# A gated-attention and MLP kernel on one core: the second half of its hand-written instruction order arranged anew, with some steps on other engines and in other buffers

## The chip, the cores and the metric

The kernel runs on one core of one Trainium2 chip. A core has a matrix engine (PE, which loads weights and multiplies), a vector engine (DVE), a scalar engine (ACT), a general engine (POOL) and a queue engine (SP) that here only issues transfers; ACT issues a few as well. Each engine works through its own instructions strictly in order and waits for the others by semaphores. The metric is the device time of one execution in microseconds, taken as the median of the runs. Lower is better.

## The reference

Four batches, eight heads, 768 time steps, head size 48. A gated linear attention comes first, and its output, with the heads laid side by side to 384 columns, goes through a low-rank mixing along time and then a two-layer MLP with a residual:

```python
for t in range(S):
    state = alpha[:, :, t, :, None] * state + np.einsum('bhd,bhe->bhde', k[:, :, t], v[:, :, t])
    y[:, :, t] = np.einsum('bhd,bhde->bhe', q[:, :, t], state)
...
xt = x.transpose(0, 2, 1)
h = xt @ U @ V
u = x + h.transpose(0, 2, 1)
ch = np.maximum(u @ w_ch1, 0.0) @ w_ch2
return (u + ch).astype(np.float32)
```

## The kernel before

Each batch is cut into six chunks of 128 time steps. Work is named by a step's short name and "batch.chunk". One chunk of attention goes like this, for the batches 2 and 3 that the prediction speaks of; the line numbers are those of the profile:

- `load` (L350, and L343 for alpha) brings alpha, k, q and v of a chunk into one of 40 `io` buffers, all issued by SP in this part of the program.
- `ln` (ACT, L549) takes the logarithm of alpha, `cum` (PE, L561 and L570) sums it along time, two chunks at once in batch 3 and in `cum1`/`cum2` steps, and `exp` and `tot` (ACT, L601, L602, L604) make the factors `ai`, `aa` and `tot` of it.
- `rv` (a plain cast of v: L265 on ACT, L269 on POOL), `rk` and `rq` (L612 on DVE or POOL) scale k and q. They write one of four `rkq` buffers.
- `tkq` (L637) transposes both by a transfer that SP issues, into one of four `kqt` buffers. This is done for all chunks of batch 2 and for 3.0 to 3.2; the other chunks of batch 3 go through PE (`tr`, L625) and copies (`kqev`, L265 or L267).
- `sc` (PE, L653, eight matmuls) makes the scores, `mask` (DVE, L663, two of them) cuts them to the causal part, `d` (PE, L676), `add` (DVE, L703) and `st` (L687, DVE or POOL) carry the state on, `y` (PE, L715 and L720) makes the output and `yev` (L265 or L267) copies it out of PSUM.

When all six chunks of a batch are done, `xu` (PE, L735), `utx` and `xs` (L750) make the low-rank product, `hb3` (PE, L760, three chunks side by side; `hb`, L771, for one) spreads it over time, `u` (DVE, L772) adds the residual for one chunk, and `tu` (L777, issued by SP) transposes the `u` of two chunks by a transfer. Then the MLP: `mlp1 b.tt.j` (PE, L820, three matmuls; tt is the half of the time steps, j one of twelve column blocks), `relu` (L830 on ACT, L832 on DVE), `mlp2 b.c.g` (PE, L846, four matmuls), `out` (DVE, L852) and `store` (L855, L857, issued by SP).

Nothing in the program is scheduled by a compiler. The functions that describe the stages only add steps to a list of 1036 with their dependences. The string `TABLE` then gives the order: each entry of three characters is the number of a step (two characters, base 64) and the engine on which it is to run (P, A, D, G for POOL, S for SP). The string `SLOTS` gives, in the order in which buffers are first used, which of a pool's slots each one takes. A step waits for what it reads, and for the last users of the slot that it writes.

```python
op = self.ops[CODE.index(table[n]) * len(CODE) + CODE.index(table[n + 1])]
for b in op.bufs:
    if b.slot is None:
        b.slot = b.pool.slots[CODE.index(next(nxt))]
op.fn({"P": "PE", "A": "ACT", "D": "DVE", "G": "POOL", "S": "SP"}[table[n + 2]])
```

Around entry 560 the program is in the MLP of batch 1, which is the filler for PE there, while the attention of batch 2 runs through its small steps; behind it the MLP of batch 2 is laid between the attention steps of batch 3, and at the end the MLP of batch 3 stands alone.

Of the kernel before, what the change touches and what calls it, by code (L numbers as in the profile page):

```python
# [34 lines left out]
LrDLqDLsSLiPJhPLoDLmDLpSJlPNDGJiDLkDLjDJmPM+GJZPJnPNJPN3PLlSN5AJaPOFPNSGNTGCRSNjANYPJbPJoDNEGNKDMPPMJPJcDNZDNUSNFSOIAMQD
NiAMRPMbPCVSCUSOHACMSNkANhAOaAMKALxPMSALyAMcDLvPN2DL-PMADLwAOKAMDPMEDOMGN4PN6DMLPMHPMIDObAOJAMMALzPN7PN8DN9DL0ANGPNVPNWD
NHDNlGLtPNIDLuDL9PNXDL1PL+AL2AOLGCOSL7PL5PMTPMUDL8DL6ANgACNSMXPMFPMNPMODCZSCYSF+SL3PNmGMGDCSSL4AONPNrPMdPNLPNbPMBPMePCWS
MYDMZPNaGNnSNMANsDOcDOdGNtDOePOOPMaDOPANwAN+PN-DOQDOfPMCAOgAMfPCaSFzSMiPNcAOhAOGGMgDOAGOUPOZGORPGKSJpSGESF-SJwSOiPNoPOVD
OSDMjPOBPOCAMnPMoPFySNqDNpDMpPNuPNvAOjDOTDOXPOYAOkDOWGOlPMkPOmAOnPMVPMsPOoAOuPMWDJdSOvDOwPO1POxDO2DGFSOySMtPOzPO0DMuPM2P
# [7 lines left out]
DCHCEABAQCSDFBTDRDGHCVCAUEADBCAWCCBAABHEDEXYGCZFABCHaEGDFbBBADBCBBHFEDBCAGEcBFCAAHAEGAFBBBBEBdGFCDBAHABeEBfghjHBEilmkCAn
BBDAFGACADBCBAFABGCBDACCDCFBGCBBDCABBBFBGDABEGHCHAEFDBCCAHAIGDAECBFDBACAHGECAACAECJBKCGDDFAAHAEMDACBDABLDFGBEPHDCNAACBCB
BCABGBBFEOCBQSTDHARGVBACAEDADHBGFACBUAWCAaZBACEDHYDCCBCFHBeEDEFCACDbABjCHFcADAAABEDfkAgCBGBHCFAEDGCBCHCAFEDBADGBCXHEBBhA
CFAnGEEDBHFGICBBABBDADAAHAEDDGCFACEAHFDEBBACABBCECCFHDBBAECAFHBEJCFKCBBAEDHFAMBGCDEFGAEBDHEGBCAHDBCANOSGUWVE  # L50
"""


# [863 lines left out]
```

## Time and profile before

| what | us |
|---|---|
| median of 3 runs | 160.28 |
| the runs | 158.03, 161.46, 160.28 |
| the profiled execution, its own time | 157.4 |
| its span, first to last instruction | 155.6 |
| PE busy in it | 145.7 |
| DVE, ACT, POOL busy in it | 107.2, 88.3, 62.2 |

The profiled execution is faster than each of the three runs, so a sum made on its rows is about an execution that waited less than the usual one. The span and the execution's own time differ by 1.8 us that lie around the program. Times "at" a point are microseconds from the span's start.

### The profile page before, as it was taken

What the parts mean: (1) busy time and instruction counts of PE and PEld (TensorE: products, weight loads), DVE (VectorE), ACT (ScalarE), POOL (GpSimd) and SP (SyncE); (2) the same over time, 40 slices, a digit from 0 to 9 for tenths busy, and PEclk for the clock granted to TensorE, in tenths of its full rate; (3) what the DMA queues carried; (4) which work ended last, traced back from release to release, by engine and by line L of the source; (5) the groups of instructions that cost most, each with busy time, mean ns of one, the idle gap of its engine ahead of it and who ended that gap; (6) DMA issues with size and microseconds to landing.
All of it is one profiled execution on the core that took longest, in us unless ns stands there. A gap on an engine that the chain in (4) does not pass through costs nothing.

```text
span 155.6 us, 4554 instructions
## 1 busy us (share of the span) xinstructions
PE 145.7 (94%) x1773; PEld 96.4 (62%) x1773; DVE 107.2 (69%) x239; ACT 88.3 (57%) x228; POOL 62.2 (40%) x100
## 2 busy tenths in 40 slices
PE   0889999999999999999996999999999999999992
PEld 0567777766676665766674656665777566666661
DVE  6169989978975568787885879479978473313251
ACT  3858878999946673776658463864442202462000
POOL 8079787448947722292253227006641000000000
PEclk9999999999999999999999999999999999999999
DMA  4999999999999999999699997899984055872142
GB/s 119 323 328 327 293 244 361 320 261 247 283 335 289 188 239 207 236 221 201 136 193 150 237 235 142 170 187 190 215 198 115 0 101 117 256 257 83 51 156 101
DMA packets 94453, 32.35 MB, mean 208 GB/s; under 512 B 88128, under 2 KB 94400, under 8 KB 94432
## 3 DMA queue, kind: packets, MB, share of 16 engines
q1 hardware_dynamic: 89152, 30.09, 81.5%
q10 hardware_dynamic: 5280, 1.97, 4.8%
q8 instruction: 14, 0.23, 0.7%
q14 instruction: 7, 0.06, 0.1%
HBM read 23.79 MB, written 4.72 MB: 183 GB/s over the span
## 4 chain that ended last, share of the span: by engine, by line
PE 66%; DMA 16%; SPq 4%; ACT 3%; DVE 3%; POOL 3%; issue 1%; POOLq 0%
PE ps L846 27%; PE ps L820 18%; DMA h1t<-in_moe_w_ch_dram 4%; DMA io<-in_alpha_dram 4%; DMA kqt<-rkq 3%; SPq L350 3%; DMA io<-in_k_dram 2%; POOL rkq L612 2%; DMA io<-in_q_dram 2%; PE ps L421 2%; PE ps L653 2%; DVE ub L772 2%; PE ps L445 2%; PE ps L720 1%; PE ps L771 1%
## 5 line engine op out<-in xcount | busy, mean ns | idle before, releaser
L846 PE MATMUL ps<-w_sb,h1t 128*128 128x384 bf16 (+2 forms) x300 | 52.1, 320 | 0.1
L820 PE MATMUL ps<-uT,w_sb 128*128 128x384 bf16 x288 | 50.6, 326 | 0.0
L846 PEld LDWEIGHTS <-h1t 128*128 128x128 bf16 x300 | 27.6, 98 | 17.0 <-issue 1.2
L820 PEld LDWEIGHTS <-w_sb 128*128 128x128 bf16 x288 | 27.0, 98 | 16.8 <-issue 0.3
L830 ACT ACTIVATE h1t<-ps 128x384 bf16<-128x384 f32 x53 | 24.4, 497 | 21.2 <-PE ps L820 20.9
L832 DVE TENSOR_SCALAR h1t<-ps 128x384 bf16<-128x384 f32 x43 | 22.9, 554 | 17.8 <-PE ps L820 16.2
L663 DVE TENSOR_TENSOR pm<-ps,maskc 128x512 bf16<-128x512 f32 x28 | 17.6, 684 | 4.8 <-PE ps L653 4.0
L852 DVE TENSOR_TENSOR io<-ub,ps 128x384 f32<-128x384 bf16 (+2 forms) x25 | 12.8, 533 | 9.0 <-PE ps L846 8.9
L612 POOL TENSOR_TENSOR rkq<-io,aa 128x384 bf16<-128x384 f32 x12 | 11.0, 915 | 15.7 <-DMA io<-in_q_dram 15.7
L612 POOL TENSOR_TENSOR rkq<-io,ai 128x384 bf16<-128x384 f32 x10 | 9.1, 914 | 13.0 <-DMA io<-in_k_dram 5.4
L265 ACT CAST xb<-ps 128x192 bf16<-128x192 f32 (+1 forms) x23 | 8.4, 404 | 9.5 <-PE ps L720 5.9
L456 DVE TENSOR_TENSOR pm<-ps,maskp 128x512 bf16<-128x512 f32 x20 | 13.2, 683 | 0.6 <-PE ps L445 0.4
L772 DVE TENSOR_TENSOR ub<-xb,ps 128x384 bf16<-128x384 bf16 x24 | 11.8, 548 | 1.9 <-PE ps L760 1.0
L404 POOL TENSOR_TENSOR rkq<-io,aa 128x384 bf16<-128x384 f32 x9 | 8.3, 922 | 6.0 <-ACT aa L397 4.0
L687 POOL TENSOR_TENSOR st<-sm,tot 128x384 bf16<-128x384 f32 x7 | 5.8, 830 | 9.6 <-DVE sm L703 9.6
L404 POOL TENSOR_TENSOR rkq<-io,ai 128x384 bf16<-128x384 f32 x9 | 8.2, 913 | 3.0 <-ACT ai L396 2.5
L265 ACT COPY kqt<-ps 128x512 bf16<-128x512 bf16 x14 | 8.3, 592 | 1.9 <-PE ps L625 1.0
L549 ACT ACTIVATE lt<-io 128x384 bf16<-128x384 f32 x14 | 7.2, 524 | 3.1 <-DMA io<-in_alpha_dram 3.1
L267 DVE COPY kqt<-ps 128x512 bf16<-128x512 bf16 x16 | 6.6, 419 | 3.0 <-ACT lt L549 1.9
L421 PE MATMUL ps<-ident,rkq 128*128 128x128 bf16 x80 | 7.7, 229 | 0.7 <-DVE pm L456 0.4
L382 PE MATMUL ps<-lt,upto 128*128 128x384 bf16 x10 | 3.8, 382 | 4.5 <-ACT lt L373 4.5
L601 ACT ACTIVATE ai<-ps 128x384 bf16<-128x384 f32 x14 | 6.7, 508 | 1.5 <-POOL st L687 1.4
(122 smaller groups left out, 213.0 us busy)
## 6 DMA issues: line engine op xcount, KB each, us to landing
io<-in_q_dram SPq DMA_DIRECT2D x24, 192.0 KB, 4.3
io<-in_k_dram SPq DMA_DIRECT2D x22, 192.0 KB, 3.9
io<-in_alpha_dram SPq DMA_DIRECT2D x20, 192.0 KB, 4.3
io<-in_v_dram SPq DMA_DIRECT2D x20, 192.0 KB, 4.1
out_dram<-io SPq DMA_DIRECT2D x13, 192.0 KB, 2.0
io<-in_moe_w_ch_dram SPq DMA_DIRECT2D x12, 192.0 KB, 4.9
h1t<-in_moe_w_ch_dram SPq DMA_DIRECT2D x4, 576.0 KB, 7.1
out_dram<-io SPq DMA_DIRECT2D x20, 96.0 KB, 2.2
```

What stands on the lines that cost most here:

```text
L265: nc.scalar.copy(dst, src)
L404: eng.tensor_tensor(jh(dst()[:, :, 0:D]), raw(a), jh(x()), op=ALU.mult)
L421: nc.tensor.matmul(dst, lhsT=ring()[:, HP * j + 2 * a : HP * j + 2 * a + 2, :].rearrange("t h w -> t (h w)"), rhs=ident, start=True, stop= ...
L456: nc.vector.tensor_tensor(dst, s2, maskp.to_broadcast([C, 2, 2, C]), op=ALU.mult)
L612: eng.tensor_tensor(dst()[:, :, 0:D], a(), x(), op=ALU.mult)
L663: nc.vector.tensor_tensor(pm()[:, :, par, :], s2, maskc.to_broadcast([C, HP, C]), op=ALU.mult)
L772: P.add(f"u {b}.{c}", lambda e, c=c, hb=hb: nc.vector.tensor_tensor(ub()[:, c, :], xb()[:, c, :], hb()[:, 0:DM], op=ALU.add), r=[hb] + xk( ...
L820: nc.tensor.matmul(hb()[:, 0:TW], lhsT=w1_sb[:, ct, jt * 128 : (jt + 1) * 128], rhs=u_half(uT, ct, tt, b in QUEUE_U), start=(ct == 0), sto ...
L830: nc.scalar.activation(dst, hb()[:, 0:TW], AF.Relu)
L832: nc.vector.tensor_scalar_max(dst, hb()[:, 0:TW], 0.0)
L846: nc.tensor.matmul(hb()[:, 0 : hi - lo], lhsT=h1()[:, jt, c * C : (c + 1) * C], rhs=w2_sb[:, jt, lo:hi], start=(jt == 0), stop=(jt == NJ - 1),
L852: P.add(f"out_{hi - lo} {b}.{c}", lambda e, hb=hb, lo=lo, hi=hi: nc.vector.tensor_tensor(flat(ou)[:, lo:hi], ub()[:, c, lo:hi], hb()[:, 0 ...
```

## The change

Only the two strings are edited. The set of steps is the same 1036 (with the same four warm-up matmuls), and the first 560 entries are untouched; in the profiled execution entry 560 is issued at 70.2 us. Behind it the order of the steps on PE, ACT, DVE and POOL is new in three stretches: up to the `xu` step of batch 2; from there to the first `mlp1` step of batch 2; and from there, through the attention of batch 3, to the fourth `mlp1` step of batch 3. At each of these three points the same steps stand ahead on PE as before, and behind the last one PE's order is the old one. On SP the order of the transfers is the same as before throughout.

38 steps change their engine. Of those between the entry and the `xu` of batch 2: `rq 2.3`, `rk 2.4` and `st 2.2` go from DVE to POOL, `rv 2.2` and `rv 2.5` from ACT to POOL, `rv 2.3` from POOL to ACT, `st 2.1` from POOL to DVE; `yev` and `relu` steps are exchanged between ACT and DVE. Later `rk 3.3`, `st 3.2` and `rv 3.2` go to POOL, `rv 3.0` to ACT, `st 3.3` to DVE, and some twenty `relu`, `kqev` and `yev` steps change between ACT and DVE. Many buffers take other slots.

Two of the lines of the diff, one of the order and one of the slots:

```diff
-B2SGDDFxDJWDJPPJTPJFPJGAKYPJJPJUDI5PJRPJSAJKALAACDSK2DKKDI9PI+AJDPCASIxPB9SIyAKZDI1PI2AJQDKGPI6DJEDLCPKIDLGALHALVAKoPKHD
+GDDFxDJPPJQDKKDI-PI9PJTPJUDJDPJEDLAAJAAJWDKGPJJPI+AI5PKYPJKDI6AJRPIrPKHDKZDKIDJSAIsAIpPIqAJFPJGALCPLUALVALGAK2GKaDKVPKoP
...
-AcADBGCBCAAEHDdBGBCeBDFBfAHEgCChGDBiHBjBFAAEkBCDCABGBAlHmFACDEnACADACBGFBBECCDFEAGADGHIBJKMLCBOPABAFCDNAABHAAFBDCDEAFBGA
+AcADBGCBCAAEHDdBCBFeBGDBfAHCgCChEGBiHBjBDAACkBFGCABEBAlHmDACDCnAFAGACBEDBBCCFDFEAEAGGHIBJKMLCBOPABADFGNAABHAADBGFDCADBEA
```

Three places are shown in the order of the instructions, before and then after. A name with a number is a buffer; equal instructions that follow each other are one row.

The first is PE just ahead of `sc 2.5`, the scores of the last chunk of batch 2. Before, its weights and columns come from `kqt_188`, and `mlp2` matmuls (L846) stand ahead of it:

```order
L846 LDWEIGHTS h1t_73
L846 MATMUL ps<-w_sb,h1t_73 128x384
L846 LDWEIGHTS h1t_73
L846 MATMUL ps<-w_sb,h1t_73 128x384
L653 LDWEIGHTS kqt_188
L653 MATMUL ps<-kqt_188 128x128
```

After, `sc 2.5` reads `kqt_190`, and the rows ahead of it are those of `sc 2.4`, which reads `kqt_189`:

```order
L653 LDWEIGHTS kqt_189
L653 MATMUL ps<-kqt_189 128x128
L653 LDWEIGHTS kqt_189
L653 MATMUL ps<-kqt_189 128x128
L653 LDWEIGHTS kqt_190
L653 MATMUL ps<-kqt_190 128x128
```

The four `mlp2`, four `d` and four more `mlp2` matmuls that stood between the two chunks' scores are now elsewhere.

The second is POOL in the same part of the program. Before, behind `rk 2.3` (first row): `st 2.1`, `rk 2.5`, `rq 2.4`, `rv 2.3`, `rq 2.5`, `st 2.3`.

```order
L612 TENSOR_TENSOR rkq_79<-io_165,ai_181 128x8x48
L687 TENSOR_TENSOR st_198<-sm_194,tot_185 128x384
L612 TENSOR_TENSOR rkq_81<-io_140,ai_182 128x8x48
L612 TENSOR_TENSOR rkq_78<-io_135,aa_177 128x8x48
L269 CAST rv_172<-io_141 128x384
L612 TENSOR_TENSOR rkq_81<-io_142,aa_179 128x8x48
L687 TENSOR_TENSOR st_197<-sm_194,tot_184 128x384
```

After, behind the same `rk 2.3`: `rq 2.3`, `rv 2.2`, `rk 2.4`, `rk 2.5`, `rq 2.4`, `st 2.2`, `rq 2.5`, `rv 2.4`.

```order
L612 TENSOR_TENSOR rkq_79<-io_167,ai_181 128x8x48
L612 TENSOR_TENSOR rkq_79<-io_132,aa_178 128x8x48
L269 CAST rv_176<-io_134 128x384
L612 TENSOR_TENSOR rkq_81<-io_137,ai_182 128x8x48
L612 TENSOR_TENSOR rkq_78<-io_140,ai_180 128x8x48
L612 TENSOR_TENSOR rkq_81<-io_135,aa_177 128x8x48
L687 TENSOR_TENSOR st_199<-sm_195,tot_186 128x384
L612 TENSOR_TENSOR rkq_78<-io_142,aa_179 128x8x48
L269 CAST rv_173<-io_143 128x384
```

`rq 2.3`, `rv 2.2`, `rk 2.4` and `st 2.2` have come to POOL, and `rv 2.3` and `st 2.1` have left it.

The third is DVE at the end of batch 2's attention, from the copy `utx 2` on. Before, `rk 3.3` stands behind it, and the `u` steps (L772) run over the chunks 5, 4, 3, 2, 1, 0, with an `out` step of batch 1 (L852) ahead of the last two:

```order
L267 CAST utx_206<-ps 96x384
L612 TENSOR_TENSOR rkq_80<-io_150,ai_180 128x8x48
L772 TENSOR_TENSOR ub_205<-xb_202,ps 128x384 x4
L852 TENSOR_TENSOR io_162<-ub_204,ps 128x384
L772 TENSOR_TENSOR ub_205<-xb_202,ps 128x384 x2
```

After, the six `u` steps follow each other and run over the chunks 1, 2, 3, 4, 5, 0:

```order
L267 CAST utx_206<-ps 96x384
L772 TENSOR_TENSOR ub_205<-xb_202,ps 128x384 x6
L852 TENSOR_TENSOR io_162<-ub_204,ps 128x384
L687 TENSOR_TENSOR st_196<-ps,tot_185 128x384
L703 TENSOR_TENSOR sm_194<-ps,st_196 128x384
```

On PE `hb3 2.0`, which makes the sums for the chunks 0 to 2, now stands ahead of `hb3 2.3` for the chunks 3 to 5, where before it stood behind it. The order of the three transposes on SP is still `tu 2.5` (chunks 4 and 5), `tu 2.3`, `tu 2.1`.

More of the change, by code (lines that the diff above doesn't have):

```diff
@@ L30 @@
 KiAIoAK0AKEGKkAKhAKjAIjPFwPJ+AIcDIdDIePKlGKmGIkDB8SJLPJBPJHPJCAKxAJMDKFSKnSKSGKTGK1GM8AIfDKyAJNPJIDJXPKJPJVPLBAJOAJYAKUS
-B2SGDDFxDJWDJPPJTPJFPJGAKYPJJPJUDI5PJRPJSAJKALAACDSK2DKKDI9PI+AJDPCASIxPB9SIyAKZDI1PI2AJQDKGPI6DJEDLCPKIDLGALHALVAKoPKHD
-KVPKWDKqDKpDLEALUALFAKgAKaGB6SJxPJyPCBSJzPJ2PKrPI3PLWGIrPKXDK3SLJGKLPKbPJ3PIsDLIDKuPB+SLKSI4AKwGLXGKvALYSI-PJAAM7AKsDJ0D
-KMDKtDJ4PKcAI7PK7PIpPIqAI8AIzPI0AJ5DK4PNeACCSK8DM9PNAANBANOAK6DK5DM-ANPAK9GNCALLPLDGJrPLOPCLSLMDLNDLPDCJSCQSCKSJsPLZPLaD
-LbDJtPJuDLRPCGSIvPK+PLTAK-DLQGLcPItPIuDIwDLSANdANRANQALdALePLfANfPNxALgPN0ANzACESLhDCXSNyAJfPCISCTSOEAODAJgPN1DLnPCFSNNA
@@ L35 @@
[L35 to L39, printed above, removed]
@@ L40 @@
-OpPOqDOrPMqDO3SM3PM4PMxPMyPOsDMzPPkPMvDM5DPlDOtSJjSPcPPYPPZAPiPPaPPbAPjAPCPPAPPBAPQPMlDM0DPKPO8PPLDO+PO6PPGPO7APdAPRDPUP
+GDDFxDJPPJQDKKDI-PI9PJTPJUDJDPJEDLAAJAAJWDKGPJJPI+AI5PKYPJKDI6AJRPIrPKHDKZDKIDJSAIsAIpPIqAJFPJGALCPLUALVALGAK2GKaDKVPKoP
+KpDB2SCDSKgGCASLEAKXDKqDM7AJ2PJ3PI7PI8DI1PB9SLIGI2DLWGKrPLFALJGIxPKuPB6SCBSKsDKWDKvAKwALHAJ4PJrPKLPJ5DKMANeAJxPIyDK3SM9P
+M-ANAANOANPAK4PKbPK7PNCAKcAK6DK5DKtGLXGK8DB+SLDGK9GLKSJyPJzPLYSNQANBAK+PK-AIzPI0ALOPItPJ0DLPDIuACCSCLSNdALQGLLPLMDLNDCJS
+LZPJsPLTGNRALaDIvPJtPIwACQSLbDLRPLcPLdALSDI3PI4ACKSJuDLePCGSNfPLfALgPLhDN0ANzAJfPJgPNxANyALiPLkDLmDCESLnPLoDLqDLrDLjDJhP
@@ new lines @@
+CXSN1GNDGCISM+ANSGJZPJaPJlPNJPNNACTSJmPCFSNhALsSLpSNEGNTGN3PNYPJiDODAOEANiANKDNZDJnPJbPJcDN5AOFPOaAMRPMXPMHPObALlSCRSJoD
+MYANjAMVPMJPMWDN2DOHAMIALvPMKALzPMDPMEDOKAMSAMNPMODN4PLwAMLPL0ANkAMMDL5POIANUSOJAN6AL6AMTPMUANFSCVSN7PN9DN8DNVPNGPL3PNXD
+L4ANWDMFPL1PL2AMGANHDOMGLxPMZPMaAL-PL7PL9PNIDMAANbPL+ANcACUSCMSNlGCOSLyDNaGOLGNgGOOPOQAL8DMPPNLPNrPNsDONPNMAMQAOPDLtPMbP
+McACNSNmGCZSOdGCYSMBPF+SCSSCWSOcDNnSCaSFzSORPOePMsPNtGLuDOSDOfPNwAGKSJpSOgAN+PGESOGGF-SOTDJwSMCAOhAMtPN-DOADOBPOUPOVDNoP
+NpDNqDOiPOCAFySJdSGFSOWGOkDMiPOjDMjPOXPM2POYANuPOZGOlPOmAMnPNvDOnPM3PM4POoAOwPOuPM5DOxDOvDOySO1POzPO0DO2DO3SMuPMoPMxPOpP
@@ L41 @@
+OrPMkPMdPMePMvDOqDMfPMyPOsDOtSMpPJjSPYPPZAPkPPlAMgDMqDMzPPcPPiPPaPPbAPjAPCPPAPPBAPQPMlDM0DPKPO8PPLDO+PO6PPGPO7APdAPRDPUP
 PMPGQSF4SO4PPDAO5APIPO-DPOPPJDPVAO9APSPPmPPEPM6SPgPPNAPTAPhDPWPPePPfDMmSJvSM1SPPAJqSGLSMrSJkSPXAGRSF5SMhSJ6SJ1SPyPQGPP3P
@@ L45 @@
 ABCDEAFAGBBHCIJCAAAABKABCLAMDBENAFOCGPCBHBBQDEACRCAAHBSGCDEBTAHCBUBDBDVFCHWBACDBDBXCEGDFACCADHCYDEFZCAAaCAbBGBDHCFABCAEH
-AcADBGCBCAAEHDdBGBCeBDFBfAHEgCChGDBiHBjBFAAEkBCDCABGBAlHmFACDEnACADACBGFBBECCDFEAGADGHIBJKMLCBOPABAFCDNAABHAAFBDCDEAFBGA
[L47 to L50, printed above, removed]
+AcADBGCBCAAEHDdBCBFeBGDBfAHCgCChEGBiHBjBDAACkBFGCABEBAlHmDACDCnAFAGACBEDBBCCFDFEAEAGGHIBJKMLCBOPABADFGNAABHAADBGFDCADBEA
+GCHFCABAQCSDDBTDRGEHFVCAUCADBCAWCCBAABHCGEXYECZDABFHaCEGDbBBADBFBBHDCGBFECAcBDCAAHAACADBBBBCBdADCDBAHABeCBfhjgHBCilkmCAn
+BBDADAECAGBFBADEBACBDAFCGCFBAFBBDCABBBDBAGABEGFAHECDCBFHAECDBAGHABACACECDFCCHEICAAGHBDDADACFJKBCAHBMCDAFEBBCAAGCBCCDALBB
+CDDGABCNBPOACFDBQGAEABSCFDTRGVAEBBABCACFHDCUGBEWCBaCDHDGDZYACBEeBABAAbBFCBGEBAgcAAHDCCEBCHDGCCAECfABCFHDGCBEBAAACHFBEAmh
+DXDADDCGHBAFBnjBAECHAFDGHCBBABCBEACFDBHGAEAACBFDHDGAFBEHIAAGFDEHFDGBCJKEHFAGCBLBDFHGBCHEFAHBEDCAFEDCPOVBSTUH
 """
```

## The prediction

> **What bounds the kernel now.** I read the page first, then PE's busy time by stretches, then the list of waits, and at last the timeline around the wait that was left. The page says that PE is the engine that counts, at full clock throughout:
>
> ```profile
> span 155.6 us, 4554 instructions
> ...
> PE 145.7 (94%) x1773; PEld 96.4 (62%) x1773; DVE 107.2 (69%) x239; ACT 88.3 (57%) x228; POOL 62.2 (40%) x100
> ...
> PEclk9999999999999999999999999999999999999999
> ```
>
> The next view gives stretches (start:end and length), then the busy time of PE, PEld, DVE, ACT and POOL with counts. Entry 560 comes at 70, so the change can only touch what lies behind:
>
> ```profile
> 70.00:82.45 12.45, 12.45 (x141) 8.08 (x141) 10.18 (x20) 7.41 (x19) 4.12 (x6) 1.00 0.93 176
> 82.45:84.69 2.24, 0.91 (x35) 0.83 (x34) 1.29 (x2) 2.24 (x8) 1.13 (x2) 1.00 1.30 95
> 84.69:129.00 44.31, 44.31 (x479) 28.48 (x480) 33.84 (x65) 20.43 (x51) 12.78 (x16) 1.00 0.82 165
> 129.00:152.70 23.70, 23.65 (x158) 14.81 (x155) 8.73 (x18) 6.39 (x15) 0.00 (x0) 1.00 0.48 149
> ```
>
> PE is busy for the whole of every stretch but one. In 82.45 to 84.69 it works 0.91 of 2.24 us. So behind entry 560 there is one wait of 1.33 us, and no more than that can be won in this execution: the steps are the same and PE has no other hole. The list of waits (who, for whom; total, times, longest) names it, and shows that ACT and DVE, with their `relu` steps, wait for PE and not the other way:
>
> ```profile
> ACT h1t L830 <- PE ps L820: 20.9, 15, 8.4
> DVE h1t L832 <- PE ps L820: 16.2, 16, 2.4
> ...
> PE ps L653 <- DMA kqt<-rkq: 1.3, 1, 1.3
> ```
>
> The timeline of PE there (start, length, instruction):
>
> ```profile
> 82.45 0.40 PE L653 MATMUL ps<-kqt 48*128 48x128 bf16 x8
> 82.68 0.50 PE L561 MATMUL ps<-lt,trij 64*128 64x192 bf16 x8
> ...
> 84.68 0.40 PE L653 MATMUL ps<-kqt 48*128 48x128 bf16 x8 [1.33 <-DMA kqt<-rkq]
> 85.01 0.82 PE L846 MATMUL ps<-w_sb,h1t 128*128 128x384 bf16 x4
> 85.84 0.81 PE L846 MATMUL ps<-w_sb,h1t 128*128 128x384 bf16 x4
> 86.59 0.40 PE L653 MATMUL ps<-kqt 48*128 48x128 bf16 x8
> ```
>
> These are `sc 2.3`, `cum2 3.0`, the wait, `sc 2.4`, `mlp2`, `mlp2` and `sc 2.5`. `sc 2.4` waits for its transpose `tkq 2.4`.
>
> **Part one: the wait at sc 2.4, minus 1.33.** The change moves `cum2 3.0` and other filler ahead of `sc 2.3`, and `d 2.4`, `mlp2 1.3.0`, `mlp1 1.0.2` and `y 2.3` between `sc 2.3` and `sc 2.4`. What the transposes need is next; SP first (the last two rows are from the transfer view and the chain: time from issue to landing of the transpose issued at 80.95, and of that at 79.57), then POOL and DVE:
>
> ```profile
> 76.66 1.83 SPq L637 DMA_TRANSPOSE kqt<-rkq  x1
> 78.53 0.58 SPq L350 DMA_DIRECT2D io<-in_v_dram  x1
> 79.57 2.62 SPq L637 DMA_TRANSPOSE kqt<-rkq  x2
> 80.95 1.24 SPq L637 DMA_TRANSPOSE kqt<-rkq  x1
> ...
> kqt<-rkq SPq DMA_TRANSPOSE x1, 4.7
> ...
> 79.57 5.07 DMA kqt<-rkq
> ```
>
> ```profile
> 76.79 0.91 POOL L612 TENSOR_TENSOR rkq<-io,ai 128x384 bf16<-128x384 f32 x1 [4.57 <-DMA io<-in_k_dram]
> 77.66 0.91 POOL L612 TENSOR_TENSOR rkq<-io,aa 128x384 bf16<-128x384 f32 x1
> 78.52 0.50 POOL L269 CAST rv<-io 128x384 bf16<-128x384 f32 x1
> 79.46 0.91 POOL L612 TENSOR_TENSOR rkq<-io,aa 128x384 bf16<-128x384 f32 x1 [0.44 <-DMA io<-in_q_dram]
> 82.31 0.83 POOL L687 TENSOR_TENSOR st<-sm,tot 128x384 bf16<-128x384 f32 x1 [1.94 <-DVE sm L703]
> 78.74 0.69 DVE L612 TENSOR_TENSOR rkq<-io,ai 128x384 bf16<-128x384 f32 x1
> ```
>
> Before, `tkq 2.4` could go at 79.57 because `rk 2.4` ran on DVE until 79.43. On POOL `rk 2.4` stands ahead of `rk 2.5`, in the 4.57 us in which POOL waited for k of 2.5, so it costs nothing there, and so do `rq 2.3` and `rv 2.2` in the same hole. `rq 2.4` keeps its time, about 77.6 to 78.5. SP is free at 78.53 + 0.58 = 79.11, so `tkq 2.4` goes at about 79.15, 0.4 earlier, and lands at 79.15 + 5.07 = 84.2. PE comes to `sc 2.4` some 0.33 (one `sc`, the distance 84.68 to 85.01) ahead of `sc 2.5`, whose place I work out below as 84.96, so at 84.6. The 1.33 go in full, with 0.4 to spare; had it landed at 84.64 as before, less than 0.1 would stay.
>
> **Part two: a new wait at sc 2.5, plus 0.26.** It now follows `sc 2.4` directly. Its place on PE comes from what stands ahead of it. Only before: `mlp2 1.3.1` (85.84 to 86.59, 0.75) and one `mlp1`; only after: another `mlp1` and `y 2.3`. The `mlp1` cancel; `y` has these two rows, from the chain:
>
> ```profile
> 87.74 0.17 PE ps L715 x4
> 87.91 0.20 PE ps L720 x8
> ```
>
> So it is 0.37 minus 0.75, minus 0.38; I take minus 0.3, since part of the 0.75 may be the change from one kind of matmul to the next, which would stay. PE is there at 86.59 - 1.33 - 0.3 = 84.96. The transpose needs `rq 2.5`, which waits for its q and ends at 79.46 + 0.91 = 80.37 as before; `st 2.2`, new on POOL ahead of it, takes 0.83 from about 78.5 and is over at 79.3, covered by that wait with 0.1 to spare. Before, SP came to `tkq 2.5` only at 80.95, held by the one at 79.57; now it can at about 80.45. With the same 4.7 it lands at 85.15, and the wait with the semaphore is about 0.26. Bounds: 0 if it lands 0.3 sooner; 85.65 - 84.96 and a semaphore, 0.75, if its landing stays where it was. I take 0.26, since both steps ahead of it go earlier.
>
> **Part three: a new wait at the first mlp1 of batch 2, plus 0.65.** The rows are `hb3 2.3` and the first `mlp1` of batch 2 on PE, the `u` steps on DVE, the three `tu` on SP, the second of them alone, and its time to landing:
>
> ```profile
> 92.42 0.50 PE L760 MATMUL ps<-utx,vm_sb 32*128 32x384 bf16 x6
> 98.69 1.63 PE L820 MATMUL ps<-uT,w_sb 128*128 128x384 bf16 x9
> ...
> 92.80 1.95 DVE L772 TENSOR_TENSOR ub<-xb,ps 128x384 bf16<-128x384 bf16 x4 [0.56 <-PE ps L760]
> ...
> 93.85 3.88 SPq L777 DMA_TRANSPOSE uT<-ub  x3
> 95.16 1.24 SPq L777 DMA_TRANSPOSE uT<-ub  x1
> ...
> uT<-ub SPq DMA_TRANSPOSE x1, 2.8
> ```
>
> The first `mlp1` steps are of the second half of time and need the chunks 2 to 5, so `tu 2.5` and `tu 2.3`. Before, these landed by 95.16 + 2.8 = 97.96, and PE came at 98.69: 0.7 to spare. PE does the same steps ahead of this point in both orders, so it now comes at 98.69 - 1.33 = 97.36. `hb3` comes 1.33 earlier too, at 91.09, and the first `u` 0.38 behind it (92.80 - 92.42), at 91.47. But chunk 5 is now the fifth `u` and not the first, and SP's first transpose needs chunks 4 and 5. A `u` follows the last by (1.95 - 0.55) / 3 = 0.47, so it ends at 91.47 + 4 x 0.47 + 0.55 = 93.9, where the second `u` before ended at 93.82. `tu 2.5` goes when it went before, 93.9, and PE waits 97.96 - 97.36 and a semaphore: 0.65. A wait in part two shifts both sides alike and takes nothing from this. Bounds 0.5 and 0.9, for a tenth or two on each of those steps.
>
> **All else at nothing.** The `relu`, `yev` and `kqev` copies go between two engines that the list of waits shows idle for 20.9 and 16.2 us behind PE; their cover is that idle time, and if it is gone a PSUM bank comes free late. SP's transfers stand in the same order, so each load goes when it went, but those behind the three `tu` wait in SP for `u 2.5` as well. They keep their times while PE is some 0.4 earlier. `ln 3.0` goes on ACT ahead of the last `exp` of 2.4 and so puts this alpha in front of `rq 2.4`:
>
> ```profile
> 70.80 0.62 SPq L343 DMA_DIRECT2D io<-in_alpha_dram  x1
> ...
> io<-in_alpha_dram SPq DMA_DIRECT2D x1, 192.0 KB, 5.2
> ```
>
> It lands at 76.0, the `exp` is done near 77, and `rq 2.4` starts at 77.6: covered by half a microsecond. In the third stretch PE had no wait (44.31 of 44.31), so nothing is to be won; POOL, which takes on `rk 3.3`, `rv 3.2` and `st 3.2` there, is busy for 12.78 of it and DVE for 33.84, so I find nothing to lose either, as long as the loads keep their times.
>
> **The sum.** -1.33 + 0.26 + 0.65 = -0.42. On the profiled execution this is 157.4 to 157.0; that execution is 2.9 below the median, and on the median it is 160.28 to 159.9. With the ends of the new waits, 0 and 0.5, or 0.75 and 0.9, it is 159.45 to 160.6.
>
> **The rivals.** *The gain stays whole:* the new order's transposes land early enough and only part one is left, 160.28 - 1.33 = 158.95. For it speaks that landing times are loose:
>
> ```profile
> DMA to landing us min/median/max: 3.0/4.3/7.3
> ...
> DMA to landing us min/median/max: 3.2/3.7/5.1
> ```
>
> (q loads, then `kqt` transposes: 4.7 is far above 3.7). Against it stands part three, whose transposes all take 2.7 to 2.8 with nothing else moving.
>
> *Slower:* q of 2.5 lands later than recorded. Before, `tkq 2.5` had 86.59 - 85.65 = 0.94 to spare; now it has none. From 0.42 late the new waits outweigh the 1.33; at 0.94 late the new order is 0.52 behind, 160.8, and later than that both pay alike. The row above, 3.0 to 7.3, says that such lateness happens; the three runs, all slower than the profiled one, say it too. The loads behind `tu 2.5` would be late with it and could add some tenths, up to about 161.5. The Trainium skill (DMA: Bandwidth & Descriptors, "Latency and other measured facts") has a rule against an order fitted to landings: the memory's share of a transfer's fixed cost is 0.2 us on average and 2 us at high load. By that, an estimate, this q could be 1.8 later and the time would be the 160.8 of this rival; the spread of the q loads here agrees with it in kind.
>
> *Faster by more than 2%:* in the usual execution, 2.9 above the profiled one, the wait at `sc 2.4` is larger and the new order hides it. It needs 3.2 in all, so 1.9 more than the recorded wait, all in this half, though the new order has 0.4 to spare there: below 157.1. PE has no wait elsewhere behind 70 that would speak for it.
>
> **How the numbers follow.** Two per cent is 3.2 us here, about what a measurement of this kernel can tell from no change. The forecast, most of the gain given back, has 0.48 and gives 159.9. The whole gain has 0.20 (158.95), the late q 0.17 (160.8 to 161.5). Faster by over 2% has 0.09 and a new wait that I don't see, worth over 3.2, has 0.06. The runs shown lie 158.03 to 161.46 for one kernel, so either middle case can stray past 2%, which moves 0.02 more to each side: faster 0.11, within 2% 0.81, slower 0.08. The range that leaves out no more than 2 in 10 reaches 1.4 below the whole gain and to the upper end of the late q: 157.5 to 161.6.
>
> **What would show it.** Right: no idle time on PE near 82 to 84; a row L653 near 85 with a few tenths of idle time put down to `kqt`; a row L820 near 98 with some 0.6 put down to `uT`, and the first L777 near 94; else PE full from 70 on. Wrong: a wait of PE over 1 us behind 100, put down to `io`, `rkq` or ACT; a wait for `kqt` as long as before; no wait for `uT`; or spans that differ by more than 1.5 us with the same idle time of PE behind 70, which would put the cause into the untouched half.

## The result, and the profile after

| | kernel before | changed kernel |
|---|---|---|
| median, us | 157.48 | 158.81 |
| lowest and highest, us | 156.55, 161.46 | 157.42, 162.67 |
| runs | 22 | 22 |
| ratio to before, 95% interval | | 1.0064 [1.0037, 1.0090] |
| the profiled execution's own time, and its span | 157.4, 155.6 | 159.83, 158.0 |

The change makes the kernel slower, by 0.64% or 1.0 us (0.6 to 1.4), which is within the 2% called no change. With more runs the median of before is 157.48 and no longer 160.28, so what counts from here is the difference and not the absolute time. The ratio leaves out the executions that ran in a slower state, for both kernels alike, so it is less than the 1.33 between the two medians.

The head of the page of the changed kernel:

```profile
span 158.0 us, 4561 instructions
...
PE 147.1 (93%) x1773; PEld 96.4 (61%) x1773; DVE 102.7 (65%) x228; ACT 91.9 (58%) x235; POOL 65.2 (41%) x104
```

The span is 2.4 us longer, but not all of that is the change's. The first PE step behind entry 560 starts at 69.36 in this execution and at 67.79 in that of before; 1.57 us were lost in entries that are the same in both. (In before, entry 560 itself is a transfer that SP issues at 70.2; PE is ahead of it.) So I count from that step, which the timeline shows inside a longer row, and cut where both orders have the same steps behind them: at `xu 2`, at the first `mlp1` of batch 2, and at `mlp1 3.1.9`, the fourth `mlp1` of batch 3. Each length is the distance between the starts of these steps in the trace, and the rest goes to the start of PE's last step.

| stretch of PE, us | before | after | difference |
|---|---|---|---|
| first: to `xu 2` | 21.98 | 21.51 | -0.47 |
| second: to the first `mlp1` of batch 2 | 8.93 | 9.69 | +0.76 |
| third: to `mlp1 3.1.9` | 31.83 | 32.28 | +0.45 |
| the rest, the same order in both | 21.72 | 21.72 | 0.00 |

PE's busy time by stretches after the change has the same columns as before:

```profile
70.00:85.00 15.00, 14.78 (x184) 9.59 (x182) 11.67 (x22) 10.01 (x26) 7.50 (x10) 1.00 1.27 189
85.00:100.00 15.00, 14.60 (x179) 9.06 (x177) 10.42 (x21) 9.18 (x25) 6.66 (x8) 1.00 0.87 181
100.00:131.00 31.00, 30.26 (x302) 19.42 (x303) 20.29 (x38) 14.79 (x36) 8.25 (x11) 1.00 0.76 154
131.00:154.00 23.00, 23.00 (x148) 14.23 (x146) 8.33 (x16) 6.87 (x16) 0.00 (x0) 1.00 0.45 145
```

The one hole of 1.33 us has become four smaller ones: three of the four stretches now miss 0.22, 0.40 and 0.74. PE's own waits, from the list of waits:

```profile
PE ps L820 <- DMA uT<-ub: 0.7, 1, 0.7
PE ps L653 <- DMA kqt<-rkq: 0.5, 2, 0.3
PE ps L625 <- DVE rkq L612: 0.2, 1, 0.2
```

The timeline of PE puts them in their places:

```profile
76.33 0.62 PE L653 MATMUL ps<-kqt 48*128 48x128 bf16 x16 [0.22 <-DMA kqt<-rkq]
...
87.42 0.40 PE L653 MATMUL ps<-kqt 48*128 48x128 bf16 x8 [0.26 <-DMA kqt<-rkq]
...
90.88 0.50 PE L735 MATMUL ps<-xb,u_sb 128*32 128x384 bf16 x6
...
100.56 0.81 PE L820 MATMUL ps<-uT,w_sb 128*128 128x384 bf16 x4 [0.70 <-DMA uT<-ub]
...
115.23 0.40 PE L625 MATMUL ps<-ident,rkq 128*128 128x128 bf16 x4 [0.18 <-DVE rkq L612]
```

These are `sc 2.1`, `sc 2.5`, `xu 2`, the first `mlp1` of batch 2, and `tr 3.5`. `sc 2.4` doesn't wait any more. The waits at `sc 2.5` and at `mlp1` are the two that the prediction named, with 0.26 and 0.70 where it had 0.26 and 0.65. The wait at `tr 3.5` is in the third stretch, which the prediction put at nothing. So most of the prediction's own signs of being right stand in this trace (no hole at `sc 2.4`, a few tenths at `sc 2.5`, some 0.6 for `uT`), and the kernel is slower all the same; the sign that failed is "else PE full from 70 on". The one at `sc 2.1` hangs on a transpose that came late out of the disturbed first part of this execution; in none of the other executions told of below does it stand.

### The profile page after: what moved, and what is told of

It is laid out like the page before. It is cut to its first block, busy times and chain, and to the rows that moved or that the text cites. A ratio compares the mean times of both kernels' runs of the same rounds, so it can differ in the third digit from the quotient of the medians.

```text
span 158.0 us, 4561 instructions
## 1 busy us (share of the span) xinstructions
PE 147.1 (93%) x1773; PEld 96.4 (61%) x1773; DVE 102.7 (65%) x228; ACT 91.9 (58%) x235; POOL 65.2 (41%) x104
## 4 chain that ended last, share of the span: by engine, by line
PE 59%; DMA 18%; DVE 6%; SPq 6%; POOL 4%; ACT 3%; issue 3%; POOLq 0%; DVEq 0%
PE ps L846 23%; PE ps L820 16%; DMA io<-in_q_dram 7%; SPq L350 5%; POOL rkq L612 3%; DVE ub L772 3%; DMA io<-in_k_dram 3%; DMA kqt<-rkq 3%; PE ps L421 3%; DMA io<-in_alpha_dram 2%; DMA uT<-ub 2%; DMA out_dram<-io 2%; PE ps L528 2%; PE ps L445 1%; PE ps L771 1%
## 5 line engine op out<-in xcount | busy, mean ns | idle before, releaser
L846 PE MATMUL ps<-w_sb,h1t 128*128 128x384 bf16 (+2 forms) x300 | 52.0, 320 | 0.0
L830 ACT ACTIVATE h1t<-ps 128x384 bf16<-128x384 f32 x60 | 28.0, 495 | 20.0 <-PE ps L820 19.6
L846 PEld LDWEIGHTS <-h1t 128*128 128x128 bf16 x300 | 27.4, 98 | 16.9 <-issue 1.5
L832 DVE TENSOR_SCALAR h1t<-ps 128x384 bf16<-128x384 f32 x36 | 19.2, 554 | 15.5 <-PE ps L820 15.1
L852 DVE TENSOR_TENSOR io<-ub,ps 128x384 f32<-128x384 bf16 (+2 forms) x25 | 12.9, 535 | 13.7 <-PE ps L846 13.5
L612 POOL TENSOR_TENSOR rkq<-io,aa 128x384 bf16<-128x384 f32 x13 | 11.8, 912 | 15.3 <-ACT h1t L830 8.1
L612 POOL TENSOR_TENSOR rkq<-io,ai 128x384 bf16<-128x384 f32 x12 | 10.9, 912 | 9.2 <-ACT ai L601 5.9
L772 DVE TENSOR_TENSOR ub<-xb,ps 128x384 bf16<-128x384 bf16 x24 | 11.6, 550 | 1.4 <-PE ps L760 1.4
L269 POOL CAST rv<-io 128x384 bf16<-128x384 f32 x13 | 6.5, 500 | 10.4 <-DMA io<-in_v_dram 10.4
L404 POOL TENSOR_TENSOR rkq<-io,aa 128x384 bf16<-128x384 f32 x9 | 8.2, 919 | 5.9 <-DMA io<-in_q_dram 5.6
L404 POOL TENSOR_TENSOR rkq<-io,ai 128x384 bf16<-128x384 f32 x9 | 8.1, 908 | 5.0 <-ACT ai L396 3.8
L265 ACT COPY kqt<-ps 128x512 bf16<-128x512 bf16 x15 | 8.9, 593 | 1.6 <-PE ps L421 1.1
```

Of the source, the lines that this page charges most:

```text
L265: nc.scalar.copy(dst, src)
L404: eng.tensor_tensor(jh(dst()[:, :, 0:D]), raw(a), jh(x()), op=ALU.mult)
L612: eng.tensor_tensor(dst()[:, :, 0:D], a(), x(), op=ALU.mult)
L772: P.add(f"u {b}.{c}", lambda e, c=c, hb=hb: nc.vector.tensor_tensor(ub()[:, c, :], xb()[:, c, :], hb()[:, 0:DM], op=ALU.add), r=[hb] + xk( ...
L830: nc.scalar.activation(dst, hb()[:, 0:TW], AF.Relu)
L832: nc.vector.tensor_scalar_max(dst, hb()[:, 0:TW], 0.0)
```

## The experiments

Each was timed against the kernel before on the same chip. "Stretches" are the three of the table above, so that what the trace of one execution shows can be set beside the ratio; before has 21.98, 8.93 and 31.83. A hybrid keeps the one order up to a point where the same steps are behind both, and the other order from there on. In the short diffs a line is a step and its engine, and a minus and a plus stand at the old and the new place.

| kernel | ratio, 95% interval | stretches |
|---|---|---|
| the changed kernel again | 1.0077 [1.0040, 1.0114] | 21.11, 9.91, 32.82 |
| first part new | 0.9951 [0.9918, 0.9984] | 20.84, 9.14, 32.81 |
| second part new | 1.0091 [1.0054, 1.0128] | 21.64, 9.81, 32.91 |
| old order of `u` | 1.0075 [1.0034, 1.0115] | 21.46, 10.70, 32.18 |
| old order of `u` with its banks | 0.9988 [0.9948, 1.0027] | 20.86, 9.22, 32.65 |
| POOL edits undone | 1.0009 [0.9971, 1.0047] | 21.28, 9.69, 32.42 |
| first part new, `rk 3.4` earlier | 0.9967 [0.9929, 1.0006] | 20.91, 9.19, 31.83 |
| only `u` as in the change | 1.0037 [0.9997, 1.0078] | 21.90, 9.70, 31.89 |
| `u` and POOL undone | 1.0020 [0.9981, 1.0059] | 21.77, 9.65, 32.29 |
| both undone, `sc 2.5` later | 0.9999 [0.9958, 1.0039] | 20.92, 9.02, 32.29 |
| `rv 3.2` on ACT | 1.0063 [1.0031, 1.0096] | 21.24, 9.70, 32.63 |
| `st 3.2` on DVE | 1.0052 [1.0017, 1.0088] | 20.84, 9.92, 32.78 |

### The change in two halves

The change was run again, and cut at `xu 2` into two kernels, each with one half of it.

```diff
 entries 0 to 559
-entries 560 to 702 (to xu 2), old
+entries 560 to 702 (to xu 2), new
 entries behind: old            (second part new: the other way round)
```

> The changed order once more, for a second trace. Theory A (the new order pays back its gain in its second part): PE waits about 0.26 us at sc 2.5, 0.70 us at the first mlp1 of batch 2 and 0.2 to 0.4 us at tr 3.5 behind a long rk 3.5 on DVE, and none of over 0.2 us between entry 560 and sc 2.5; ratio to before 1.005 to 1.008. Theory B (the new order's first part is exposed to late landings, and that alone makes it slower): waits for kqt in 70 to 88 us add up to 1 us or more; same ratio.

> New order from entry 560 to the xu step of batch 2 (entry 702), old order behind it. Theory A: the 1.4 us at sc 2.4 go, 0.26 at sc 2.5 come, nothing else, so about 1.0 us faster than before, ratio 0.992 to 0.995. Theory B: as slow as the whole change, ratio 1.004 or more.

> Old order up to the xu step of batch 2, new order from there on (entry 702). Theory A: the old wait of 1.3 us at sc 2.4 stays and the 0.70 at the first mlp1 of batch 2 and 0.3 to 0.5 in the attention of batch 3 come on top, about 1.1 us slower than before, ratio 1.006 to 1.009. Theory B: no slower than before, ratio 0.998 to 1.002.

The first part alone is worth -0.77 us (0.9951 of 157.5; -1.3 to -0.3), the second +1.43 (+0.9 to +2.0). The repeat confirms the sign of the whole. So the gain is there, and more than it is lost behind `xu 2`. With the first part new, the timeline of PE has the scores of 2.4 and 2.5 in one row without idle time ahead of it, but later in the same trace a wait of 0.81 at `tr 3.4`:

```profile
86.78 0.71 PE L653 MATMUL ps<-kqt 48*128 48x128 bf16 x16
...
112.05 0.40 PE L625 MATMUL ps<-ident,rkq 128*128 128x128 bf16 x4 [0.81 <-POOL rkq L612]
```

It is no part of the change: POOL stood behind a load of k in the old order, and `rk 3.4` stood behind that.

```profile
110.21 1.78 POOL L612 TENSOR_TENSOR rkq<-io,ai 128x384 bf16<-128x384 f32 x2 [3.09 <-DMA io<-in_k_dram]
```

With the second part new, the list of PE's waits has three:

```profile
PE ps L653 <- DMA kqt<-rkq: 0.9, 1, 0.9
PE ps L676 <- POOL rv L269: 0.7, 1, 0.7
PE ps L820 <- DMA uT<-ub: 0.7, 1, 0.7
```

The first is in the old half, though at `sc 2.5`: the wait of 1.3 at `sc 2.4` that was expected there did not come in this execution. The third is the one forecast; the second is new. It is `d 3.2`, which needs `rv 3.2`, and the timeline of that execution (POOL, then PE) shows why that copy is late:

```profile
108.97 0.91 POOL L612 TENSOR_TENSOR rkq<-io,ai 128x384 bf16<-128x384 f32 x1 [2.21 <-DMA io<-in_k_dram]
109.84 0.83 POOL L687 TENSOR_TENSOR st<-sm,tot 128x384 bf16<-128x384 f32 x1
110.63 0.91 POOL L612 TENSOR_TENSOR rkq<-io,ai 128x384 bf16<-128x384 f32 x1
111.49 0.50 POOL L269 CAST rv<-io 128x384 bf16<-128x384 f32 x1
...
112.05 0.33 PE L676 MATMUL ps<-rv,rkq 128*128 128x96 bf16 x4 [0.71 <-POOL rv L269]
```

`rk 3.2` waits for its k, and behind it on POOL stand `st 3.1`, `rk 3.4` and then `rv 3.2`, which takes 0.50 and ends at 111.99. Before, `rv 3.2` ran on ACT. The repeat of the change waits 0.62 at the same step.

### The order of the u steps

Two kernels take back the order of `hb3` and `u` alone; the second also gives the six sums their old exchange of PSUM banks, so that the next user of each bank finds it free as early as in the change. The third puts the change's order of `u`, with the `out` step behind the last `u` and banks to suit, into the kernel before.

```diff
-hb3 2.0, u 2.1, u 2.2, hb3 2.3, u 2.3, u 2.4, u 2.5, u 2.0
+hb3 2.3, u 2.5, u 2.4, hb3 2.0, u 2.3, u 2.2, u 2.1, u 2.0
 tu 2.5, tu 2.3, out 1.1, tu 2.1
```

> The changed kernel with one thing undone: hb3 2.3 again ahead of hb3 2.0 on PE and the six u steps of batch 2 on DVE again over the chunks 5, 4, 3, 2, 1, 0. Theory A: tu 2.5 goes 1.3 us earlier relative to xu 2, the wait of 0.70 us at the first mlp1 of batch 2 goes, and the loads that SP holds behind it come as much earlier, so 0.7 to 1.0 us less than the changed kernel, ratio to before 0.999 to 1.002. Theory B: the wait goes and comes back at the next transfer, ratio 1.004 to 1.008.

> The changed kernel with the u order undone once more, and the six PSUM banks of hb3 exchanged with it, so that the bank which is freed first is again the one that mlp2 1.0.0 takes. Theory C (the late tu 2.5 costs 0.70 us at the first mlp1 of batch 2 and holds the loads of batch 3 behind it in SP): no wait of PE at mlp1 2.1.6 and none at mlp2 1.0.0, tu 2.5 about 1.4 us sooner behind xu 2 than in the changed kernel, ratio to before 0.999 to 1.003. Theory D (the wait only moves on, since batch 3 is bound by its loads): PE reaches the attention of batch 3 sooner and waits there for as much, ratio 1.004 to 1.008.

> The kernel before with one part of the change alone: hb3 2.0 ahead of hb3 2.3 and the u steps of batch 2 over the chunks 1, 2, 3, 4, 5, 0, with the out step behind them and the banks exchanged to suit. Theory C: tu 2.5 goes 1.4 us later, of which PE had 0.7 to spare, so a wait of 0.6 to 0.8 us for uT at the first mlp1 of batch 2, and ratio 1.004 to 1.009 with the loads behind it late. Theory D: batch 3 takes the wait up, ratio 0.998 to 1.003.

The first miss taught something: the wait at `mlp1` went, and another came. PE in that execution:

```profile
94.79 1.46 PE L846 MATMUL ps<-w_sb,h1t 128*128 128x384 bf16 x8 [1.62 <-DVE ub L772]
```

An `mlp2` wanted the bank of a sum that one of the last `u` steps now read. The order of the `u` steps and the banks had been chosen together, so the run says nothing of the price of the one. With the banks exchanged, the first `mlp1` (third row) follows `cum1` without idle time:

```profile
101.79 0.41 PE L561 MATMUL ps<-lt,trij 64*128 64x192 bf16 x6
102.03 0.34 PE L570 MATMUL ps<-ones,lt 64*128 64x1 bf16 x8
102.31 1.47 PE L820 MATMUL ps<-uT,w_sb 128*128 128x384 bf16 x8
```

The second stretch is 9.22, though the third is still 32.65, with a wait of 0.44 at `d 3.2`. The ratio 0.9988 [0.9948, 1.0027] lies wholly below the repeat's 1.0077 [1.0040, 1.0114]: the late `u` is a cause. The other way round, with only `u` late in the kernel before, the second stretch grows from 8.93 to 9.70, and PE waits there:

```profile
99.80 1.46 PE L820 MATMUL ps<-uT,w_sb 128*128 128x384 bf16 x8 [0.61 <-DVE io L852]
```

The name in brackets is the `out` step that this kernel has behind the last `u`; the transpose landed 0.14 ahead of it, so of the 0.61 all but that would be there for the transpose alone. Its ratio, 1.0037 [0.9997, 1.0078], has the sign of a loss; the interval just touches no change.

### What POOL took on

Three kernels relieve POOL in the third stretch of the changed kernel. The first takes `rv 3.2` and `st 3.2` back to their old engines and also puts `rk 3.4` ahead of `rk 3.2`; neither kernel has that place for it (before, it stood right behind `rk 3.2`), so this kernel is more than an undoing, whatever its name:

```diff
 POOL:
+rk 3.4
 rk 3.2
 st 3.1
-rk 3.4
-rv 3.2       (to ACT)
 rq 3.2, rq 3.5
-st 3.2       (to DVE, behind rk 3.5)
```

`rv 3.2` on ACT is that one line alone, `st 3.2` on DVE its one.

> The changed kernel with POOL relieved in the attention of batch 3: rv 3.2 back on ACT, st 3.2 back on DVE behind rk 3.5, and rk 3.4 ahead of rk 3.2. Theory C: rk 3.5 on DVE takes 0.55 to 0.8 us and not 0.8 to 1.2, PE does not wait for rv 3.2 at d 3.2 (0.6 to 0.7 in two of three traces), the 0.70 at mlp1 2.1.6 stays; ratio 1.002 to 1.006. Theory D: d 3.2 or its neighbours wait for other loads instead, ratio 1.006 to 1.009.

> The changed kernel with rv 3.2 alone back on ACT. Theory C: d 3.2 no longer waits for POOL (0.6 to 0.7 us in two of three traces), the long rk 3.5 (0.8 to 1.2 us beside POOL) stays and tr 3.5 waits 0.1 to 0.4; ratio 1.003 to 1.007.

> The changed kernel with st 3.2 alone back on DVE, behind rk 3.5. Theory C: rk 3.5 ends 0.41 us after the end of POOL's rq 3.5, no later, as in the traces in which st 3.2 is on DVE; d 3.2 still waits for rv 3.2; ratio 1.004 to 1.009.

Together the three edits take 0.7% off the repeat (1.0009 [0.9971, 1.0047] for 1.0077 [1.0040, 1.0114], ends that overlap by 0.0007), and `d 3.2` waits 0.08. Each alone gains less than can be told from nothing: 1.0063 and 1.0052. With `rv 3.2` on ACT the wait at `d 3.2` is 0.08 as well, but `rk 3.5` on DVE takes 1.30. The timeline of that execution (DVE, then POOL):

```profile
113.27 1.30 DVE L612 TENSOR_TENSOR rkq<-io,ai 128x384 bf16<-128x384 f32 x1
...
112.38 1.78 POOL L612 TENSOR_TENSOR rkq<-io,aa 128x384 bf16<-128x384 f32 x2
114.12 1.14 POOL L687 TENSOR_TENSOR st<-sm,tot 128x384 bf16<-128x384 f32 x1
```

Both POOL products end at 112.38 + 1.78 = 114.16, and `rk 3.5` ends at 114.57, 0.41 later. `st 3.2`, which starts beside its end, takes 1.14 where POOL's other `st` take 0.83. With `st 3.2` on DVE, `rk 3.5` takes 0.83 and `d 3.2` waits 0.45 for POOL's `rv`. So with either edit alone the other's cost is still there, which fits their small effects. `rk 3.4` was not moved alone in the new order, so a part of the 0.7% may be its. How the 0.7% splits is below what intervals of 0.4% to each side can tell, and stays open.

### Is the first part the best that is left?

The first part alone, with the wait at `tr 3.4` taken away by `rk 3.4` ahead of `rk 3.2`; then the whole change with `u` and POOL undone, and the same with `sc 2.5` behind one more `mlp2`.

```diff
 first part new, POOL:
+rk 3.4
 rk 3.2
-rk 3.4
 both undone, PE:
 sc 2.4
-sc 2.5
 mlp2 1.3.1
+sc 2.5
```

> New order up to the xu step of batch 2, old order behind it with one step moved: rk 3.4 ahead of rk 3.2 on POOL, since k of 3.4 lands 3 us before k of 3.2. Theory C: the wait of 0.81 us at tr 3.4, which the trace of the kernel without this edit shows behind a late k of 3.2, goes; ratio to before 0.990 to 0.995. Theory D: another load is waited for, ratio as without the edit, 0.995.

> The changed kernel with both undone: the u order of batch 2 with its banks, and on POOL rv 3.2 to ACT, st 3.2 to DVE behind rk 3.5, rk 3.4 ahead of rk 3.2. Theory C (these two hold all of the loss of the second part): no wait of PE over 0.3 us behind xu 2, and about what the first part alone gained, ratio 0.992 to 0.997. Theory E (the second part's order of matmuls is itself worse): ratio 0.998 to 1.002.

> The same, and sc 2.5 behind mlp2 1.3.1 instead of directly behind sc 2.4, so that 0.65 us of matmuls stand between them. Theory C: the 0.2 to 0.5 us at sc 2.5 go, ratio 0.990 to 0.996. Rival: mask 2.5 on DVE comes later for it and y 2.5 or xu 2 waits as long, ratio as without this edit.

In the first's trace PE waits nowhere behind entry 560, and the third stretch is the old 31.83. Its time, 0.9967, is not to be told from the 0.9951 without that edit; the wait of 0.81 came with a late k in the one execution that was traced, and says little of the others. That time misses the 0.990 to 0.995 that was expected, though the wait went. The other two miss what was expected, 0.992 to 0.997 and 0.990 to 0.996: they come to before's time, not below it. The first of them lands where it was expected if the second part's order of matmuls is itself worse, 0.998 to 1.002. Its trace also has a wait that the others mostly lack, at `d 3.1`, which needs `rk 3.1` (POOL, then PE):

```profile
95.94 0.91 POOL L612 TENSOR_TENSOR rkq<-io,ai 128x384 bf16<-128x384 f32 x1 [1.71 <-DMA io<-in_k_dram]
...
96.91 0.34 PE L676 MATMUL ps<-rv,rkq 128*128 128x96 bf16 x4 [0.56 <-ACT lt L549]
```

The view names a step on ACT that `d 3.1` doesn't read and that ends at 96.92, too late to be the cause; `rk 3.1` waited 1.71 for its k and ended at 96.85. The kernel with `st 3.2` on DVE waits 0.39 at the same step. The last has no wait for `kqt` left and is 0.5 shorter than before in its trace, with 0.46 still lost in the third stretch. So the wait at `sc 2.5` is not what keeps the change from its gain, and `u` and those three POOL edits aren't all of it either. The fastest kernel of the study is the first part new, 0.9951 [0.9918, 0.9984], and the only one whose interval lies below before.

## Why the prediction was wrong

The forecast was -0.42 us, the result is +1.0, and the trace has +0.74. By steps:

**Part one, -1.33: right.** The wait at `sc 2.4` is gone in the result and in every kernel with the new first part. Measured by itself the first part gives -0.77 (-1.3 to -0.3) where parts one and two made -1.07.

**Part two, +0.26: right.** 0.26 in the result's trace; 0 to 0.55 in the other traces that have the step there, as its two bounds had it (0 and 0.75). That the result's trace has the very number is luck.

**Part three, +0.65: right.** 0.70 in the result, 0.69 to 0.71 in four of the five other executions with the change's order on both engines and 0.14 in the fifth, in which PE had lost 0.39 at `d 3.1` just before. The two runs on `u` show that this order is the cause.

**"All else at nothing": this step failed.** It said that the third stretch had "nothing to lose either, as long as the loads keep their times", and of the loads, "They keep their times". The second part costs +1.43 (+0.9 to +2.0), of which part three explains 0.65. All ten executions with the new order behind `xu 2` have a longer third stretch, 32.18 to 32.91 against 31.83; of the three others with the old order there, two have 31.83 and 31.89, and the third has 32.81 by its late k. The runs show what was overlooked: steps given to POOL that PE soon needs, a product on DVE that is held up beside POOL, and an order of PE's steps that is itself some 0.2 longer.

*The loads don't keep their times.* SP before (the `tu` row, 93.85, is in the prediction, `xu 2` on PE came at 89.76), then after:

```profile
102.05 1.63 SPq L350 DMA_DIRECT2D io<-in_k_dram  x2
```

```profile
96.35 3.88 SPq L777 DMA_TRANSPOSE uT<-ub  x3
100.28 0.57 SPq L350 DMA_DIRECT2D io<-in_q_dram  x1
...
104.53 1.54 SPq L350 DMA_DIRECT2D io<-in_k_dram  x2
```

`tu 2.5` went 93.85 - 89.76 = 4.09 behind `xu 2`, and now goes 96.35 - 90.88 = 5.47 behind it. The loads follow it in SP's order: these two of k (for 3.4 and 3.2) go 8.2 behind `tu 2.5` in both. Counted from the first step behind entry 560 (67.79 and 69.36), this row starts at 34.26 before and at 35.17 after, 0.91 later, while PE was to be 0.4 earlier. I had written that these loads wait in SP for `u 2.5`, and put it at nothing all the same. Late loads alone are not the price, though. The same row with only `u` as in the change (its first step starts at 68.19), then with the old order of `u` and its banks (72.23):

```profile
103.72 1.53 SPq L350 DMA_DIRECT2D io<-in_k_dram  x2
...
106.28 1.85 SPq L350 DMA_DIRECT2D io<-in_k_dram  x2
```

With only `u` it starts 35.53 behind the first step, later still, and the third stretch is 31.89. With the old `u` and its banks it starts 34.05 behind, earlier than before, and the stretch is 32.65. Late loads cost time where steps that PE needs stand behind them on POOL.

*POOL takes its steps in order, and was given one that PE waits for.* I took POOL's 12.78 us busy out of 44.31 as cover. But it stood idle because it waited for loads, and what stands behind such a wait is late by all of it: `rv 3.2` behind `rk 3.2`, above. In the result's own trace k came early enough for `d 3.2` not to wait; in the repeat and in the second part alone it waited 0.62 and 0.71. Over all ten traces: with `rv 3.2` on POOL (six) the waits at `d 3.2` are 0, 0, 0.44, 0.45, 0.62 and 0.71, with it on ACT (four) 0.08 each.

*DVE and POOL hold each other up.* The wait at `tr 3.5` in the result's trace, DVE then POOL:

```profile
113.98 1.20 DVE L612 TENSOR_TENSOR rkq<-io,ai 128x384 bf16<-128x384 f32 x1
...
112.18 1.79 POOL L612 TENSOR_TENSOR rkq<-io,aa 128x384 bf16<-128x384 f32 x2
113.92 0.83 POOL L687 TENSOR_TENSOR st<-sm,tot 128x384 bf16<-128x384 f32 x1
```

`rk 3.5` starts on DVE just behind `st 3.2` on POOL and ends at 115.18, 0.43 behind that step's end (114.75). In the trace of before the same product on DVE took 0.55 (by-line view):

```profile
L612 DVE TENSOR_TENSOR rkq<-io,ai x1: 551/551/551, 111.7 to 111.7; 128x384 bf16<-128x384 f32 x1
```

From the start of `sc 3.4`, the step ahead of `tr 3.5`, to the next start PE takes 0.574 where it took 0.234 before, 0.34 more. Of this 0.24 belong to the wait: in the seven traces in which `tr 3.5` stands behind `sc 3.4` and doesn't wait, the distance is 0.33. The other 0.10 is there without a wait. The Trainium skill (SBUF — State Buffer, "Who interferes with whom") says that a DVE instruction with two inputs in SBUF contends with a GpSimd instruction that reads SBUF, and that a lock on a shared pair of ports decides it, not a slower rate for both. These rows agree with it: 0.55 becomes 1.20 and 1.30, and the end follows POOL's by 0.41 to 0.43.

*Some of it has no wait at all.* In the kernel with both undone and `sc 2.5` later, 0.22 of the 0.46 in the third stretch are steps of PE that take longer from start to start. An `mlp1` ahead of an `sc` takes 0.583 where one ahead of another `mlp1` takes 0.488, and the new order has two of them for one before. `sc 3.4` takes 0.33 ahead of `tr 3.5` where it took 0.234 ahead of another `sc`. The second place in that kernel's trace:

```profile
113.78 0.40 PE L653 MATMUL ps<-kqt 48*128 48x128 bf16 x8
114.11 0.40 PE L625 MATMUL ps<-ident,rkq 128*128 128x128 bf16 x4
```

All ten kernels with the new order behind `xu 2` have both places, so about 0.2 us of the third stretch comes with the order itself. No run takes this by itself.

**The sum.** Against the trace: the forecast's -1.07 for the first stretch came out as -0.47, of which 0.39 are the wait at `sc 2.1` and the step ahead of it, which isn't the change's. Another 0.09 is `sc 2.5`: from the start of `sc 2.4` to its own it takes 0.66, and 0.31 with the first part new and no wait, so it costs 0.35 and not the 0.26 of idle time. The remaining 0.12 no run takes by itself. The second is 0.11 above the 0.65; the third is the 0.45 that was put at nothing, 0.24 for the wait at `tr 3.5` and about 0.2 for the order without a wait. 0.60 + 0.11 + 0.45 is the 1.16 between -0.42 and +0.74.

**The rivals.** Late q at `sc 2.5` has the sign that came, but by the wrong mechanism: `sc 2.5` waits the 0.26 of a q in time, and with that wait taken away (both undone, `sc 2.5` later) the kernel still isn't faster than before. Its side remark, that the loads behind `tu 2.5` could add some tenths, pointed at the right queue, but late loads alone cost 0.06 (31.89 for 31.83, only `u` as in the change). "The gain stays whole" is true of the first part alone. "Faster by more than 2%" rested on a usual execution 2.9 above the profiled one; with 22 runs the median is 157.48, 0.1 above it.

**What stays open.** The two halves by themselves make -0.77 + 1.43 = +0.66, the whole +1.0 and its repeat +1.2; the intervals allow this. But taking back `u` with its banks (-0.9% of the repeat) and POOL's edits (-0.7%) each came out lower, the second with intervals that just overlap, and both together gave 1.0020 and not less than either; its trace has the 0.56 at `d 3.1`, which says something of that one execution only. One execution per kernel has a trace, and in it the landing of a single load moves PE by up to 0.8, so the order of the small waits can't be settled from these.

## What to carry to other kernels

An order fitted to one recorded execution can be right about each wait that it removes and still lose, because steps moved behind a late load or transpose on an engine that takes its steps in order inherit its lateness; so go through every queue behind a moved step (here SP's loads behind `tu 2.5`, POOL's `rv` behind `rk`) before any step is put at nothing. An engine that is idle because it waits for data is no free place for work that another engine needs soon. And when a change has parts that meet at a common point, time the halves: here half of it is the better kernel.

## What the hardware showed that I had not expected

- A DVE product of two SBUF inputs (L612, 128x384) took 0.55 us by itself and 0.78, 0.83, 1.20 and 1.30 beside POOL, and ended 0.41 to 0.43 behind the end of POOL's instruction. The 0.78, with the first part new and `rk 3.4` earlier (DVE, then POOL; 109.98 + 0.92 is 110.90, and the product ends at 111.31):

```profile
110.53 0.78 DVE L612 TENSOR_TENSOR rkq<-io,ai 128x384 bf16<-128x384 f32 x1
...
109.98 0.92 POOL L612 TENSOR_TENSOR rkq<-io,aa 128x384 bf16<-128x384 f32 x1
```

- POOL pays as well when it comes second: `st` took 1.14 to 1.15 in place of 0.83.
- The load of k 3.2, 192 KB, took 3.5 us from issue to landing in before, 3.8 in the change, 5.0 in its repeat, 5.1 with the second part new and 5.9 with the first part new, so it spreads by more than the whole change moves. The longest (by-line view of that execution's loads):

```profile
DMA to landing us min/median/max: 3.3/4.5/5.9
```
